# Grouped-query decode attention with a bilinear feed-forward block: query weights loaded as one chunk, output weights in two loads, gate, up and down weights in fewer pieces

## The chip, the cores and the metric

The kernel runs on one core of a Trainium2 chip. The metric is the device time of one execution in microseconds (us), the median of several runs. All data are 32-bit floats.

## What is computed

One token is decoded. The cut reference, with B = Sq = 1, D = 512, 32 query heads in 8 groups, head size 128, Sk = 65536 cached positions and F = 1792:

```python
q = (layernorm(x) @ wq)                  # 512 x 4096
p = softmax(q . k_cache * 128 ** -0.5)   # 4 query heads share one of 8 K/V heads
h = x + (p . v_cache) @ wo               # 4096 x 512
n = layernorm(h)
y = h + ((n @ w_gate) * (n @ w_up)) @ w_down
```

K and V have 268 MB each; wq and wo 8.4 MB each, gate and up together 7.3 MB, w_down 3.7 MB. Every byte is used once.

## The kernel before, in words

**Chunks.** K and V are read in 64 chunks of 128 partitions x 16384 values (8192 KB, one row of 64 KB per partition). Each of the 8 heads has four K chunks and then four V chunks. Even chunks go to the buffer `kv[0]`, odd ones to `kv[1]`. SP issues every load; before a chunk it waits for the semaphore `free`, which DVE raises when PE has finished with that buffer.

**One chunk on PE.** `windows` (L359) multiplies 32 windows of 512 columns, each with its own 32 columns of the stationary tile `st`, into four row blocks of one bank of `ps`. Each window is two matmul records in the trace, so a chunk is 64 records. A window's operand in `st` is zero but for the columns wanted, so one chunk loop serves K, V, gate and up, and w_down. PE runs one loop over a pair of chunks (`pe_pair`, `pe_chunks`, `pe_second`, `pe_rest`); two registers, head `hr` and pair `ur`, choose the branch.

**A head.** At its start (L391 to L400) PE multiplies the normalized x with the head's 1024 KB of wq (8 records), DVE copies the row `qrow`, PE turns it into columns, and DVE spreads them over `qx` and `st` (L224 to L234). The softmax runs between the K and the V chunks. At the end (`pe_sum`) PE divides out the sum, multiplies with the head's wo, and DVE adds to `acc`. The wq of the next head and the wo of this one come in one load of 2048 KB (L148), issued when DVE has raised `wf`.

**The end.** The last V chunk comes in four pieces (L158). Then SP loads gate and up into `kv[0]` in four pieces with gaps (L162, L164): 3584 of every 4096 columns are filled. It loads w_down into `kv[1]` in pieces of 6, 3, 1, 1, 1, 1 and 1 chunks of 512 columns (L167 to L172). PE and DVE do the layer norm (`pe_norm`, L295 to L315), the 32 windows of gate and up, then `pe_glu`: a matmul for the variance, four transposes of the result, and a matmul into `attn` whose result nobody reads (L430). DVE forms the products (L323 to L336). The first 9 chunks of w_down go through 12 windows, the last 5 through `final` (L370), and `add` (L479) adds `res`, which holds the window sum times the inverse deviation plus `acc` (L340). DVE copies the sum to `y` (L492) and SP stores it.

**Order.** Each engine's order is written out by hand; queues are served in order. A piece has its own semaphore; where before and after differ in the number of pieces, GpSimd raises the unused ones in advance (L133).

```python
take(pe_e, qt)
windows(0, 0, 16, s_k0)
windows(0, 16, 24, s_k16)
windows(0, 24, 28, s_k24)
windows(0, 28, 32, s_k28).then_inc(kd, 1)
```

Of the kernel before, what the change touches and what calls it, by code (L numbers as in the profile page):

```python
# [5 lines left out]
ALU = mybir.AluOpType  # L6
AX = mybir.AxisListType

P = 128
# [33 lines left out]
def body(nc, xr, kvd, wq0, wqo, wo7, gu, wd, out):  # L43
# [11 lines left out]
    sel_h, sel_q, sel_1 = (tile(n, P, w) for n, w in (("sel_h", REP), ("sel_q", 4), ("sel_1", 1)))  # L55
# [21 lines left out]
    gu_sb, uf, y = tile("gu_sb", P, 512), tile("uf", P, 2, 2, 4, 2), tile("y", P, 256)  # L77
# [18 lines left out]
    s_k0, s_k16, s_k24, s_k28 = (sem(f"s_k{i}") for i in (0, 16, 24, 28))  # L96
    s_v0, s_v8, s_v16, s_v24, s_v28 = (sem(f"s_v{i}") for i in (0, 8, 16, 24, 28))
    s_wq, s_w = sem("s_wq"), sem("s_w")
    s_wd = [sem(f"s_wd{i}") for i in range(NC - SIDE)]
    s_xr = sem("s_xr")  # L100
    late, s_act, s_pool, s_y, s_a, s_out = (sem(n) for n in ("late", "s_act", "s_pool", "s_y", "s_a", "s_out"))
    gu_t = kv[0].rearrange("p (k x) -> p k x", k=KT)[:, :, 0:2 * F]
# [18 lines left out]
    sp.dma_start(wq_sb, wq0).then_inc(s_wq, 16)  # L121
# [11 lines left out]
    for p, w, n in ((s_k16, 16, 0), (s_k24, 16, 0), (s_k28, 16, 0), (s_v8, 17, 0),  # L133
                    (s_v16, 16, -1), (s_v24, 16, -1), (s_v28, 16, -1)):
        pool_e.sem_inc(p, w * (end // 2 + n))
    for t in (o_pad, f_pad, sel_pad, acc, y):
        c_pads = pool.tick(pool_e.memset(t, 0.0))
    pool_e.wait_ge(s_act, 1).then_inc(s_pool, 1)
    pool_e.br("fin")

    even(0)
    odd(1)
    for g in range(2, 6):
        take(sp, free)
        (odd if g % 2 else even)(g)
    with nc.Fori(0, LAST, engines=SP_ONLY) as h:
        take(sp, wf)
        sp.dma_start(wqo_sb, wqo[h]).then_inc(s_w, 16)  # L148
        with nc.Fori(0, 2 * NT, 2, engines=SP_ONLY) as c:
            for i, put in enumerate((even, odd)):  # L150
                take(sp, free)
                put(c + (h * (2 * NT) + 6 + i))
    take(sp, wf)
    sp.dma_start(wo_sb, wo7).then_inc(s_w, 16)
    take(sp, free)
    even(end - 2)
    take(sp, free)
    for lo, hi, p in ((0, 16, s_v0), (16, 24, s_v16), (24, 28, s_v24), (28, 32, s_v28)):  # L158
        cs = slice(lo * 512, hi * 512)
        sp.dma_start(kv[1][:, cs], kvd[end - 1][:, cs]).then_inc(p, 16)  # L160
    take(sp, free)
    for lo, hi, p in ((0, 2, s_k0), (2, 3, s_k16)):  # L162
        sp.dma_start(gu_t[:, lo:hi], gu[:, lo:hi]).then_inc(p, 16)
    for cs, p in ((slice(0, 2048), s_k24), (slice(2048, 2 * F), s_k28)):  # L164
        sp.dma_start(gu_t[:, 3, cs], gu[:, 3, cs]).then_inc(p, 16)
    take(sp, free)
    sp.dma_start(  # L167
        wd_t[:, 0:8 * D].rearrange("p (r x) -> p r x", r=2)[:, :, 0:3 * D],
        wd[:, 0:6 * D].rearrange("p (r x) -> p r x", r=2)).then_inc(s_v0, 16)
# [39 lines left out]
    dve_e.tensor_copy(xn, ps[0][:, 0:KT]).then_inc(tok, 3)  # L209
# [3 lines left out]
    with nc.Fori(0, HKV, engines=DVE_ACT):  # L213
# [9 lines left out]
        take(dve_e, pd)  # L223
        dve_e.tensor_copy(qrow, ptp[0][0:1, :]).then_inc(tok, 1)  # L224
        take(dve_e, pd)
        dve_e.sem_inc(wf, 1)
        q4 = sm[0][:, 0:REP]
# [58 lines left out]
        for half, p in ((0, tok), (1, s_a)):  # L286
            cs = slice(half * 256, half * 256 + 256)
            dve_e.scalar_tensor_tensor(  # L288
                out=acc[:, cs], in0=attn[:, cs], scalar=1.0, in1=acc[:, cs], op0=ALU.mult, op1=ALU.add,
                accum_out=rsum[:, half:half + 1]).then_inc(p, 1)  # L290
# [4 lines left out]
    dve_e.memset(st[:, :, 0:2], 0.0).then_inc(own, 1)  # L295
# [7 lines left out]
    def centred(o, a):  # L303
# [3 lines left out]
    hj = st.rearrange("p (j k t) c -> p t k j c", j=4, k=KT)  # L307
    centred(hj[:, 0, :, :, 0], acol.unsqueeze(2).to_broadcast([P, KT, 4]))
    centred(hj[:, 1, :, 0:3, 1], acol.unsqueeze(2).to_broadcast([P, KT, 3])).then_inc(qt, 1)
# [5 lines left out]
        out=ln_s3, in0=ln_s3, scalar1=KT * EPS, scalar2=None, op0=ALU.add).then_inc(tl, 1)  # L315
    take(dve_e, kd)
    for half in range(2):
        cs = slice(half * 256, half * 256 + 256)
        dve_e.tensor_copy(gu_sb[:, cs], ps[0][:, cs]).then_inc(tl, 1)
    sj = st.rearrange("p (j r) c -> p r j c", j=4)[:, :, :, 0]  # L320
    gux = [t.rearrange("p (a b j x) -> p a b j x", a=2, b=2, j=4)[:, 0, :, :, 0:2] for t in ptp]
    take(dve_e, pd, 2)
    mine(dve_e.tensor_copy(uf[:, 0], gux[0]))  # L323
    dve_e.tensor_tensor(
        out=sj[:, 0:2, :], in0=gux[0][:, :, :, 0], in1=uf[:, 0, :, :, 1], op=ALU.mult).then_inc(qt, 1)
    dve_e.reciprocal(ln_r3, sm[0][:, 0:1])
    take(dve_e, pd)
    mine(dve_e.tensor_copy(uf[:, 1], gux[1]))
    dve_e.tensor_tensor(
        out=sj[:, 2, :], in0=gux[1][:, 0, :, 0], in1=uf[:, 1, 0, :, 1], op=ALU.mult)  # L330
    for o, g, u in ((f_pad[:, 0:1, 0], gux[0][:, 0, 3:4, 0], uf[:, 0, 1, 3:4, 0]),
                    (f_pad[:, 1:4, 0], gux[1][:, 1, 0:3, 0], uf[:, 1, 1, 0:3, 1]),
                    (f_pad[:, 4:5, 0], gux[1][:, 0, 3:4, 0], uf[:, 1, 1, 3:4, 0])):
        i = dve_e.scalar_tensor_tensor(
            out=o, in0=g, scalar=ln_r3[:, 0:1], in1=u, op0=ALU.mult, op1=ALU.mult)
    i.then_inc(s_v8, 1)  # L336
    take(dve_e, kd)
    for half in range(2):
        cs = slice(half * 256, half * 256 + 256)
        dve_e.scalar_tensor_tensor(  # L340
            out=res[:, cs], in0=ps[1][:, cs], scalar=ln_r3[:, 0:1], in1=acc[:, cs],
            op0=ALU.mult, op1=ALU.add).then_inc(tl, 1)
# [39 lines left out]

    hr, ur = (pe_e.alloc_register(n) for n in ("h", "u"))
# [5 lines left out]
    pe_e.br("pe_head")  # L389
    block("pe_head")  # L390
    pe_e.wait_ge(tok, 3)  # L391
    for k in range(KT):
        i = mm(ptp[0][0:1, :], xn[:, k:k + 1], wq_sb[:, k, :], start=(k == 0), stop=(k == KT - 1))  # L393
    i.then_inc(pd, 1)
    pe_e.wait_ge(tok, 4)
    for r in range(REP):
        i = pe_e.transpose(sm[0][:, r:r + 1], qrow[0:1, r * P:(r + 1) * P], ident[0:1, 0:1])  # L397
        if r == 1:
            i.then_inc(tok, -4)
    i.then_inc(pd, 1)  # L400
# [45 lines left out]
    windows(1, 16, 24, s_v16)  # L446
    windows(1, 24, 28, s_v24)
# [94 lines left out]
```

## Time and profile before

| what | value |
|---|---|
| median of 3 runs | 1308.67 us (1308.66 to 1308.84) |
| profiled execution, first to last instruction (span) | 1307.4 us |
| median less span | 1.27 us |
| PE busy | 686.2 us (52%) |
| DVE busy | 111.6 us (9%) |
| ACT busy | 54.9 us (4%) |
| bytes moved by DMA | 564.72 MB, 432 GB/s over the span |

The profile gives no time of its own for the profiled execution but the span, so what lies around the span is taken as the difference to the median. A row of the timeline has start, duration, engine, line, operation, the tile written and those read, the number of merged instructions, and in brackets the idle time before it with what ended it. PE is the matmul side of TensorE, PEld its weight loads. PEclk is the granted clock: 1.00 is 2.4 GHz, 0.50 is 1.2 GHz.

### The profile page before, as it was taken

The numbers are of one execution on the slowest core, as the hardware profiler recorded it, in microseconds if no ns is written. First come the engines' busy times: TensorE is split into PE (matmuls) and PEld (weight loads), VectorE is DVE, ScalarE is ACT, GpSimd is POOL, SyncE is SP. The second block draws the span as 40 slices with busy tenths as digits, with TensorE's granted clock in tenths as the row PEclk, the third lists the DMA queues.
The fourth block names the chain that finished last, engine by engine and source line by source line (L and its number), as shares of the span: only waits on it lengthen the run. The fifth ranks groups of instructions, "written<-read, shape, count | busy, mean of one in ns | idle before, by whom it ended". The sixth has DMA issues, their size and how long they took to land. (4 is left out here: it accounts for less than half of the span.)

```text
span 1307.4 us, 10833 instructions
## 1 busy us (share of the span) xinstructions
PE 686.2 (52%) x4610; PEld 191.5 (15%) x4610; DVE 111.6 (9%) x286; ACT 54.9 (4%) x106; POOL 2.7 (0%) x12
## 2 busy tenths in 40 slices
PE   4456364453654545553554636535566445545557
PEld 1011111110111111111110211101111111111112
DVE  1000010100101001000010101001010010100101
ACT  0000000000000000000000000000000000000000
POOL 0000000000000000000000000000000000000000
PEclk8676796776976768767787767868677677877679
DMA  9999999999999999999999999999999999999999
GB/s 417 421 445 429 437 447 419 449 417 449 417 449 417 449 417 449 421 445 427 439 439 427 449 417 449 417 449 417 449 417 449 417 434 440 441 437 429 447 408 382
DMA packets 12850, 564.72 MB, mean 432 GB/s; under 512 B 1409, under 2 KB 1457, under 8 KB 2610
## 3 DMA queue, kind: packets, MB, share of 16 engines
q1 hardware_dynamic: 12848, 564.71, 99.8%
q10 hardware_dynamic: 2, 0.00, 0.0%
HBM read 564.66 MB, written 0.05 MB: 432 GB/s over the span
## 5 line engine op out<-in xcount | busy, mean ns | idle before, releaser
L364 PE MATMUL ps<-kv,st 128*32 128x512 f32 x4184 | 591.0, 728 | 534.6 <-DMA kv<-in_kv 520.1
L364 PEld LDWEIGHTS ps<-kv,st 128*32 128x32 f32 x4184 | 146.7, 131 | 962.3 <-DMA kv<-in_kv 568.1
L242 DVE TENSOR_REDUCE mx<-sc 128x1 f32<-128x512 f32 x32 | 21.9, 686 | 535.9 <-DVEq L107 535.9
L414 PE MATMUL ptp<-ident,ex 128*128 128x128 f32 x128 | 27.3, 372 | 19.8 <-ACT ex L220 19.5
L216 ACT COPY sc<-ps 128x512 f32<-128x512 f32 x32 | 18.8, 586 | 444.6 <-ACTq L107 444.5
L274 DVE TENSOR_TENSOR orow<-ps,orow 128x512 f32<-128x512 f32 x16 | 11.1, 691 | 298.3 <-DVEq L107 298.3
L220 ACT ACTIVATE ex<-sc,nbias 128x512 f32<-128x512 f32 x32 | 22.8, 714 | 304.4 <-ACTq L107 304.4
L393 PE MATMUL ptp<-wqo_sb,xn 128*1 128x512 f32 x64 | 30.4, 620 | 6.4 <-DVE acc L288 5.0
L216 ACT ACT_TABLE_LOAD x8 | 10.3, 1283 | 441.5 <-ACTq L107 441.5
L261 DVE COPY st<-ptp 128x512 f32<-128x512 f32 x32 | 22.1, 692 | 44.5 <-DVEq L107 44.5
L414 PEld LDWEIGHTS ptp<-ident,ex 128*128 128x128 f32 x128 | 20.2, 188 | 22.9 <-ACT ex L220 22.8
L407 PE MATMUL sm<-ident,m 128*1 128x128 f32 x16 | 4.5, 283 | 27.2 <-DVE m L244 17.6
L277 DVE TENSOR_TENSOR orow<-ps,orow 128x256 f32<-128x256 f32 x16 | 6.0, 419 | 129.3 <-DVEq L107 129.3
L272 DVE COPY orow<-ps 128x512 f32<-128x512 f32 x8 | 5.5, 692 | 102.0 <-DVEq L107 102.0
L461 PE MATMUL attn<-wqo_sb,o_pad 128*32 128x512 f32 x64 | 8.5, 605 | 5.9 <-DVE o_pad L284 5.9
L409 PE MATMUL sm<-ones,mexp 1*128 1x1 f32 x32 | 6.9, 281 | 6.7 <-DVE mexp L251 6.7
L393 PEld LDWEIGHTS ptp<-wqo_sb,xn 128*1 128x1 f32 x64 | 4.9, 85 | 30.9 <-issue 18.1
L224 DVE COPY qrow<-ptp 1x512 f32<-1x512 f32 x8 | 5.4, 679 | 29.7 <-DVEq L107 29.7
L457 PE MATMUL ptp<-ident,orow 128*128 128x128 f32 x32 | 6.1, 300 | 3.0 <-DVE orow L277 3.0
L407 PEld LDWEIGHTS sm<-ident,m 128*1 128x1 f32 x16 | 1.3, 79 | 41.8 <-DVE m L244 24.9
L288 DVE SCALAR_TENSOR_TENSOR acc<-attn,acc 128x256 f32<-128x256 f32 x16 | 6.2, 421 | 10.8 <-DVEq L107 10.8
L397 PE MATMUL sm<-ident,qrow 1*128 1x1 f32 x32 | 3.2, 201 | 7.1 <-DVE qrow L224 7.1
(84 smaller groups left out, 78.4 us busy)
## 6 DMA issues: line engine op xcount, KB each, us to landing
wqo_sb<-in_wqo SPq DMA_DIRECT2D x7, 2048.0 KB, 32.9
kv<-in_kv SPq DMA_DIRECT2D x1, 4096.0 KB, 22.2
kv<-in_gu SPq DMA_DIRECT2D x1, 3584.0 KB, 17.6
kv<-in_kv SPq DMA_DIRECT2D x1, 2048.0 KB, 26.7
kv<-in_kv SPq DMA_DIRECT2D x2, 1024.0 KB, 29.7
kv<-in_gu SPq DMA_DIRECT2D x1, 1792.0 KB, 21.4
kv<-in_wd SPq DMA_DIRECT2D x1, 1536.0 KB, 19.0
kv<-in_wd SPq DMA_DIRECT2D x5, 256.0 KB, 20.5
```

The lines of the kernel that those rows point to most:

```text
L216: act_e.copy(sc[s], ps[s % 2]).then_inc(ad, 1)
L220: act_e.activation(ex[s - n], sc[s], AF.Exp, bias=nbias[:, 0:1], scale=SCALE, accum_out=sums[:, s:s + 1]).then_inc(atok[s - n], 1)
L242: dve_e.tensor_reduce(out=mx[:, s:s + 1], in_=sc[s], axis=AX.X, op=ALU.max).then_inc(own, 1)
L261: dve_e.tensor_copy(st[:, :, 0:16].rearrange("p g (b h) -> p b g h", h=REP), ptp[n % 2].rearrange("p (b g h) -> p b g h", b=4, h=REP)).the ...
L274: mine(dve_e.tensor_tensor(out=orow, in0=ps[n % 2], in1=orow, op=ALU.add))
L288: dve_e.scalar_tensor_tensor(out=acc[:, cs], in0=attn[:, cs], scalar=1.0, in1=acc[:, cs], op0=ALU.mult, op1=ALU.add, accum_out=rsum[:, hal ...
L364: i = mm(ps[buf][32 * j:32 * j + 32, :], st[:, 8 * j + r, :], kv[buf][:, w * 512:(w + 1) * 512], start=(r == 0), stop=(r in (2, 3, 7)), sk ...
L393: i = mm(ptp[0][0:1, :], xn[:, k:k + 1], wq_sb[:, k, :], start=(k == 0), stop=(k == KT - 1))
L409: mm(sm[0][:, 0:1], mexp.rearrange("p g h -> p (g h)"), ones[0:1, 0:1], start=True, stop=True).then_inc(pd, 1)
L414: i = pe_e.transpose(ptp[half][:, b * P:(b + 1) * P], ex[half][:, b * P:(b + 1) * P], ident)
L457: i = pe_e.transpose(ptp[1][:, b * P:(b + 1) * P], orow[:, b * P:(b + 1) * P], ident)
L461: i = mm(attn[32 * r:32 * r + 32, :], o_pad[:, r, :], wo_sb[:, r, :], start=True, stop=True)
```

## The change

- **Query weights.** All of wq is one chunk of 8192 KB, the first load into `kv[1]`. It goes through the chunk loop once ahead of the heads: `st` gets the normalized x (`diagonal(0)`), the eight rows of queries come out of one bank, and a new PE block `pe_pick` turns and gathers them with `sel_8` into `q_all`. The heads lose their q matmuls, the row copy and the transposes. The second K chunk is issued only when wq has left `kv[1]` (an added wait on `free`).
- **Output weights.** wo comes in two loads of 4096 KB, heads 0 to 3 at the start and 4 to 7 when DVE has raised `wf` four times. GpSimd waits for each and raises `tw` by four. PE picks one of four quarter tiles by the register `wr`.
- **Gate and up** are packed without gaps, at windows 4 to 31 of `kv[0]`, in two pieces of 20 and 8 windows. `pe_pick` replaces the transposes of `pe_glu`; the unread matmul L430 is gone. The variance matmul moves ahead of the gate and up windows, and two matmuls there put `acc` into `pva`.
- **w_down** comes in pieces of 8, 3, 2 and 1 chunks; 11 chunks go through the windows, 3 through `final`. `res` is now a plain copy, because the inverse deviation is multiplied into the products.
- **Last V chunk** in two pieces instead of four.

```diff
-SIDE = 9
+SIDE = 11
-    sp.dma_start(wq_sb, wq0).then_inc(s_wq, 16)
+    sp.dma_start(kv[1], wq).then_inc(s_v0, 16)
...
     even(0)
+    take(sp, free)
     odd(1)
-    for g in range(2, 6):
-        take(sp, free)
-        (odd if g % 2 else even)(g)
-    with nc.Fori(0, LAST, engines=SP_ONLY) as h:
-        take(sp, wf)
-        sp.dma_start(wqo_sb, wqo[h]).then_inc(s_w, 16)
-        with nc.Fori(0, 2 * NT, 2, engines=SP_ONLY) as c:
+    for half, pairs in ((0, end // 4), (1, end // 4 - 2)):
+        if half:
+            take(sp, wf, HKV // 2)
+        sp.dma_start(wo_sb, wo[half]).then_inc(s_wo, 16)
+        with nc.Fori(0, 2 * pairs, 2, engines=SP_ONLY) as c:
             for i, put in enumerate((even, odd)):
                 take(sp, free)
-                put(c + (h * (2 * NT) + 6 + i))
+                put(c + (2 + half * (end // 2) + i))
...
+    pieces((0, 16, 32), 0, kv[1], kvd[end - 1], (s_v0, s_v16))
+    pieces((0, 20, 28), 4, kv[0], gu, (s_k0, s_k24))
+    pieces((0, 8, SIDE), 0, wd_t, wd, (s_v0, s_v8))
+    for lo, hi, p in ((SIDE, NC - 1, s_wd[0]), (NC - 1, NC, s_wd[1])):
+        sp.dma_start(wd_t[:, (lo + 1) * D:(hi + 1) * D], wd[:, lo * D:hi * D]).then_inc(p, 16)
...
+    dve_e.tensor_copy(diagonal(0), spread(ps[0][:, 0:KT], 8)).then_inc(qt, 1)
+    take(dve_e, kd, 2)
+    dve_e.sem_inc(free, 1)
+    columns(ps[1])
+    mine(dve_e.tensor_copy(q_all, picked.rearrange("p b c -> p c b")))
...
     take(pe_e, qt)
-    windows(0, 0, 16, s_k0)
-    windows(0, 16, 24, s_k16)
-    windows(0, 24, 28, s_k24)
-    windows(0, 28, 32, s_k28).then_inc(kd, 1)
-    pe_e.br_eq(hr, HKV, on_true="pe_glu", on_false="pe_second")
+    windows(0, 0, 24, s_k0)
+    windows(0, 24, 32, s_k24).then_inc(kd, 1)
+    pe_e.br_eq(hr, HKV, on_true="pe_pick", on_false="pe_second")
```

How the instructions move is shown at three places. First SP's loads from the start into the steady loop (`in_` is the DRAM tensor, the size is partitions x values). Before:

```order
L121 DMA wqo_sb<-in_wq 128x2048
L116 DMA kv<-in_kv 128x16384
L119 DMA kv<-in_kv 128x16384
L116 DMA kv<-in_kv 128x16384
L119 DMA kv<-in_kv 128x16384
L116 DMA kv<-in_kv 128x16384
L119 DMA kv<-in_kv 128x16384
L146 UNCONDITIONAL_BRANCH
L148 ISA
L148 DMA wqo_sb<-in_wqo 128x4096
```

Changed:

```order
L118 DMA kv<-in_wq 128x16384
L113 DMA kv<-in_kv 128x16384
L116 DMA kv<-in_kv 128x16384
L147 DMA wo_sb<-in_wo 128x8192
L148 UNCONDITIONAL_BRANCH
L113 ISA
L113 DMA kv<-in_kv 128x16384
```

The load of wq is eight times as long and shares its buffer with the second K chunk; the load per head is gone, and a load of 4096 KB stands once ahead of each half of the chunks. Second, SP's last loads. Before:

```order
L160 DMA kv<-in_kv 128x8192
L160 DMA kv<-in_kv 128x4096
L160 DMA kv<-in_kv 128x2048 x2
L163 DMA kv<-in_gu 128x2x3584
L163 DMA kv<-in_gu 128x3584
L165 DMA kv<-in_gu 128x2048
L165 DMA kv<-in_gu 128x1536
L167 DMA kv<-in_wd 128x2x1536
L170 DMA kv<-in_wd 128x1536
L172 DMA kv<-in_wd 128x512 x5
```

Changed:

```order
L158 DMA kv<-in_kv 128x8192 x2
L158 DMA kv<-in_gu 128x10240
L158 DMA kv<-in_gu 128x4096
L158 DMA kv<-in_wd 128x4096
L158 DMA kv<-in_wd 128x1536
L165 DMA kv<-in_wd 128x1024
L165 DMA kv<-in_wd 128x512
```

Fifteen loads became eight. Third, PE behind the last windows of w_down, up to the end (`pva` holds the result, `f_pad` the products). Before:

```order
L374 MATMUL pva<-kv,f_pad 32x256 [waits s_wd0]
L374 MATMUL pva<-kv,f_pad 32x256
L374 MATMUL pva<-kv,f_pad 32x256 [waits s_wd1]
L374 MATMUL pva<-kv,f_pad 32x256
L481 MATMUL pva<-res,sel_pad 32x256 [waits tl]
L374 MATMUL pva<-kv,f_pad 32x256 [waits s_wd2]
L374 MATMUL pva<-kv,f_pad 32x256
L481 MATMUL pva<-res,sel_pad 32x256 [waits tl]
L374 MATMUL pva<-kv,f_pad 32x256 [waits s_wd3]
L374 MATMUL pva<-kv,f_pad 32x256
L488 UNCONDITIONAL_BRANCH
L374 MATMUL pva<-kv,f_pad 32x256 [waits s_wd4]
```

Changed:

```order
L372 MATMUL pva<-kv,f_pad 32x256 [waits s_wd0]
L372 MATMUL pva<-kv,f_pad 32x256 x3
L377 MATMUL pva<-res,sel_pad 32x256 [waits tl] x2
L486 UNCONDITIONAL_BRANCH
L372 MATMUL pva<-kv,f_pad 32x256 [waits s_wd1]
L372 MATMUL pva<-kv,f_pad 32x256
```

The two additions of `res` now stand directly ahead of the last chunk's matmuls, where three chunks' matmuls, two of them with waits, used to stand behind the first addition.

## Rows read from the trace of the kernel before

**Rows 1.** the page: its DMA line by slices, and the packets of the whole span.
```profile
DMA  9999999999999999999999999999999999999999
...
DMA packets 12850, 564.72 MB, mean 432 GB/s; under 512 B 1409, under 2 KB 1457, under 8 KB 2610
```
**Rows 2.** windows, middle of the span; at the end PEclk, DMA share, GB/s.
```profile
600.00:1100.00 500.00, 257.92 (x1755) 72.47 (x1755) 39.91 (x95) 21.52 (x43) 0.00 (x0) 0.75 1.01 435
```
**Rows 3.** timeline, PE, chunks 0, 1, 5 and 6: start, us, what, idle before.
```profile
24.92 9.39 PE L364 MATMUL ps<-kv,st 128*32 128x512 f32 x64 [9.20 <-DMA kv<-in_kv]
...
44.26 9.96 PE L364 MATMUL ps<-kv,st 128*32 128x512 f32 x64 [9.95 <-DMA kv<-in_kv]
...
121.65 8.81 PE L364 MATMUL ps<-kv,st 128*32 128x512 f32 x64 [9.40 <-DMA kv<-in_kv]
...
145.87 8.65 PE L364 MATMUL ps<-kv,st 128*32 128x512 f32 x64 [11.12 <-DMA kv<-in_kv]
```
**Rows 4.** DMA issues: how many, KB each (left out: 8192), median us to landing.
```profile
wqo_sb<-in_wqo SPq DMA_DIRECT2D x7, 2048.0 KB, 32.9
...
kv<-in_kv SPq DMA_DIRECT2D x63, 29.3
...
kv<-in_wd SPq DMA_DIRECT2D x5, 256.0 KB, 20.5
```
**Rows 5.** the chain that ended last: start, us, what.
```profile
1280.60 18.98 DMA kv<-in_wd
...
1305.37 0.42 DVE y L492
```
**Rows 6.** timeline, PE and its weight loads, last value chunk to the end.
```profile
1271.46 8.77 PE L364 MATMUL ps<-kv,st 128*32 128x512 f32 x64 [2.10 <-PEq L107]
...
1278.86 0.13 PEld L364 LDWEIGHTS ps<-kv,st 128*32 128x32 f32 x4 [0.39 <-DMA kv<-in_kv]
...
1287.36 3.64 PE L364 MATMUL ps<-kv,st 128*32 128x512 f32 x32 [2.26 <-DMA kv<-in_gu]
...
1291.59 1.92 PE L364 MATMUL ps<-kv,st 128*32 128x512 f32 x16 [0.59 <-DMA kv<-in_gu]
...
1294.04 1.06 PE L364 MATMUL ps<-kv,st 128*32 128x512 f32 x8 [0.52 <-DMA kv<-in_gu]
...
1295.94 1.06 PE L364 MATMUL ps<-kv,st 128*32 128x512 f32 x8 [0.84 <-DMA kv<-in_gu]
...
1299.62 2.88 PE L364 MATMUL ps<-kv,st 128*32 128x512 f32 x24 [0.30 <-DMA kv<-in_wd]
...
1301.44 0.16 PEld L364 LDWEIGHTS ps<-kv,st 128*32 128x32 f32 x8 [0.80 <-DMA kv<-in_wd]
...
1302.32 1.08 PE L374 MATMUL pva<-kv,f_pad 128*32 128x256 f32 x8
...
1304.64 0.20 PEld L374 LDWEIGHTS pva<-kv,f_pad 128*32 128x32 f32 x4 [0.23 <-DMA kv<-in_wd]
```
**Rows 7.** page, part 5: the heads' q matmuls: busy, mean ns | idle before.
```profile
L393 PE MATMUL ptp<-wqo_sb,xn 128*1 128x512 f32 x64 | 30.4, 620 | 6.4 <-DVE acc L288 5.0
```
**Rows 8.** timeline, DVE, the normalization, gate/up and the residual.
```profile
1286.74 0.15 DVE L314 TENSOR_SCALAR ln_s<-ln_s 128x1 f32<-128x1 f32 x1
...
1297.21 0.76 DVE L319 COPY gu_sb<-ps 128x256 f32<-128x256 f32 x2 [10.31 <-DVEq L107]
...
1298.60 0.17 DVE L324 TENSOR_TENSOR st<-ptp,uf 128x8 f32<-128x8 f32 x1
...
1302.71 0.88 DVE L340 SCALAR_TENSOR_TENSOR res<-ps,ln_r,acc 128x256 f32<-128x256 f32 x2 [3.07 <-DVEq L107]
```
**Rows 9.** windows around the last value chunk and the gate/up stage.
```profile
1272.40:1275.80 3.40, 3.40 (x24) 1.15 (x20) 0.00 (x0) 0.00 (x0) 0.00 (x0) 0.54 0.94 400
...
1287.30:1297.00 9.70, 7.69 (x65) 1.73 (x65) 0.00 (x0) 0.00 (x0) 0.00 (x0) 1.00 1.00 425
1297.00:1299.50 2.50, 1.95 (x9) 0.90 (x8) 1.69 (x10) 0.00 (x0) 0.00 (x0) 1.00 1.01 423
```

More of the change, by code (lines that the diff above doesn't have):

```diff
@@ L40, in tick, with body @@
         return self.n
-def body(nc, xr, kvd, wq0, wqo, wo7, gu, wd, out):
+def body(nc, xr, wq, kvd, wo, gu, wd, out):
     pe_e, dve_e, act_e, pool_e, sp = nc.tensor, nc.vector, nc.scalar, nc.gpsimd, nc.sync
@@ L208, in body, with diagonal, spread, columns @@
     take(dve_e, pd)
-    dve_e.tensor_copy(xn, ps[0][:, 0:KT]).then_inc(tok, 3)
+    def diagonal(lo):
+        return bass.AP(tensor=st.tensor, offset=33 * lo, ap=[list(st.ap[0]), [256, KT], [33, 8 - lo]])
+    def spread(a, n):
+        return a.unsqueeze(2).to_broadcast([P, KT, n])
+    def columns(src):
+        for half in range(2):
+            cs = slice(half * 256, half * 256 + 256)
+            dve_e.tensor_copy(gu_sb[:, cs], src[:, cs]).then_inc(tl, 1)
+        take(dve_e, pd)
+    picked = ptp[0][:, 0:32].rearrange("p (b c) -> p b c", b=4)
+    dve_e.tensor_copy(diagonal(0), spread(ps[0][:, 0:KT], 8)).then_inc(qt, 1)
[3 more added lines that the diff above has]
+    mine(dve_e.tensor_copy(q_all, picked.rearrange("p b c -> p c b")))
     o_blocks = bass.AP(tensor=ptp[1].tensor, offset=0, ap=[list(ptp[1].ap[0]), [1, REP], [132, 4], [32, 4]])
     qd = qx.rearrange("p (j x) -> p j x", j=4)
-    with nc.Fori(0, HKV, engines=DVE_ACT):
+    with nc.Fori(0, HKV, engines=DVE_ACT) as head:
         for s in range(NT):
@@ L222, in body @@
                     accum_out=sums[:, s:s + 1]).then_inc(atok[s - n], 1)
[L223 to L227, printed above, removed]
+        q4 = q_all[:, head, :]
         dve_e.tensor_copy(
@@ L285, in body @@
         take(dve_e, pd)
-        for half, p in ((0, tok), (1, s_a)):
+        dve_e.sem_inc(wf, 1)
+        for half in range(2):
             cs = slice(half * 256, half * 256 + 256)
@@ L318, in body @@
         cs = slice(half * 256, half * 256 + 256)
[L319 to L342, printed above, removed]
+        dve_e.tensor_copy(res[:, cs], ps[1][:, cs]).then_inc(tl, 1)
     dve.n += 1
@@ L388, in body @@
     pe_e.reg_mov(hr, 0)
-    pe_e.br("pe_head")
-    block("pe_head")
[L391 to L400, printed above, removed]
+    pe_e.reg_mov(wr, 0)
+    pe_e.reg_mov(ur, 2 * NT)
+    pe_e.br("pe_second")
+    block("pe_pick")
+    for b in range(4):
+        if b % 2 == 0:
+            pe_e.wait_ge(tl, 1 + b // 2)
+        i = mm(ptp[0][:, 8 * b:8 * b + 8], gu_sb[:, b * P:(b + 1) * P], sel_8, start=True, stop=True)
+        if b == 2:
+            i.then_inc(tl, -2)
+    i.then_inc(pd, 1)
+    pe_e.br_lt(hr, HKV, on_true="pe_head", on_false="pe_second")
+    block("pe_head")
     pe_e.reg_mov(ur, 0)
@@ L474, in body @@
     mm(sm[1][:, 0:2], neg_mean, rsum, start=True, stop=True).then_inc(pd, 1)
+    for g in range(2):
+        add(g, acc, True)
+    pe_e.wait_ge(tok, 1)
+    mm(sm[0][:, 0:1], mean_m, ln_s3, start=True, stop=True).then_inc(pd, 1)
     pe_e.br_eq(hr, HKV, on_true="pe_chunks", on_false="pe_other")
```

181 lines of the change are left out of this document (87 added, 94 removed).

## The prediction

> **What bounds the kernel now.** I read the page first. The DMA engines are at nine tenths or more in every slice, and 564.72 MB moved in 12850 packets [rows 1]. The windows confirm it: from 600 to 1100 us the DMA share is 1.01 at 435 GB/s [rows 2]. Next comes PE at the landings. Chunks 0 and 1 start on PE 19.34 us apart (24.92, 44.26), each behind an idle time of over 9 us that ended with the chunk's DMA [rows 3]. So a chunk of 8192 KB passes in 19.34 us, 2.42 us per 1024 KB, and PE needs only 8.65 to 9.96 us for it. A chunk lands 29.3 us after its issue [rows 4]. Less the 19.34 us of its own transfer, about 10 us of other loads are still ahead of it when it is queued. PE, DVE and ACT work in the shadow of the loads. The time is the bytes at that pace, a start and a tail. The change moves the same bytes, so only three things can move the time: the pace of small loads, a hole in the queue, and the work after the last landing.
>
> The tail is in the chain that ended last: the loads of w_down from 1280.60, then PE, then DVE's copy to `y` at 1305.37 [rows 5]. The last load's weights start on PE at 1304.64 [rows 6]. I call that landing E; the copy starts at E + 0.73. I count back from E below.
>
> **The loads.** Before there are 87 loads: 1 of wq, 63 whole chunks, 4 pieces of the last, 7 of wqo, 1 of wo, 4 of gate and up, 7 of w_down. After there are 74: 1 + 63 + 2, 2 of wo, 2 and 4. What a load costs beyond its bytes shows at the end, where each landing has a PE row: 1287.36, 1291.59, 1294.04, 1295.94, 1299.62, 1301.44, and the last at 1304.64 [rows 6]. Between the first and the last, 10 loads with 1792 + 1024 + 768 + 1536 + 768 + 5 x 256 = 7168 KB took 17.28 us. At the chunks' pace that is 16.92 us, so a load costs 0.036 us more. One wqo load between two chunks agrees: 121.65 to 145.87 is 24.22 us [rows 3], against 24.18 for 10240 KB. Thirteen loads fewer save 13 x 0.036 = **0.5 us**. Bounds from single loads there: the one of 1792 KB cost nothing, the third one of gate and up 0.09 us. That gives a saving from 0 to 1.2 us. I take the mean, since the loads removed are of all these kinds.
>
> The Trainium skill's page "DMA: Bandwidth & Descriptors" (Anatomy of one DMA) gives each DMA a fixed cost of about 2.0 us beside its bytes. By that, 13 loads fewer would save 26 us. Here the trace disagrees: five loads of 256 KB [rows 4] landed in 1304.64 - 1301.44 = 3.20 us, 0.64 us each.
>
> **The start.** The 1024 KB of wq and chunk 0 had landed by 24.92; at 2.42 us per 1024 KB the loads began at about 3.2. After, wq lands at 22.5. PE takes up to 9.96 us for a chunk [rows 3], so SP issues the second K chunk at about 33. Chunk 0 holds the DMA engines until 41.9. So the added wait on `free` has 9 us of cover and costs nothing. Behind it on SP are the first load of wo and the chunk after; neither is late, as they are queued before the second K chunk has landed. The wait on `wf` in the middle stands behind chunk 33 on SP. When it begins, chunk 32 is in flight with about 10 us to go and chunk 33 is whole. The head's last steps, which it waits for, lie within the 6.66 us counted below from the last V matmul to `ln_s`. Nothing there either. GpSimd waits for wo and has nothing else to do until the end.
>
> **The heads.** They lose the q matmuls (64 records, 30.4 us of busy time in all [rows 7], 3.8 us a head), the row copy and the transposes. All of it lies inside waits of over 9 us for the next chunk: worth nothing. An earlier `free` only queues a load earlier behind one that is running.
>
> **The last stages, counted from E.** With 2.42 us per 1024 KB and 0.036 us per load, the changed loads land at E - 0.64 (12 and 13 of the 14 chunks of w_down), E - 1.89 (9 to 11), E - 3.74 (the first eight), E - 8.61 and E - 13.48 (gate and up), and the last V chunk at E - 25.60.
>
> - *Last V chunk.* Before, the last of four pieces landed at 1278.86, four windows were left, and the matmuls ended at 1271.46 + 8.77 = 1280.23, E - 24.41 [rows 6]. After, 16 windows (32 records) follow the last landing: 3.64 us by the row with 32 records, so E - 21.96, later by 2.45.
> - *Norm.* `ln_s` was ready at 1286.89 [rows 8], 6.66 us after the last V matmul. After that is E - 15.30, and the variance matmul now ahead of gate and up adds about 0.5. PE is ready at E - 14.8, 1.3 us before the first piece lands. No cost.
> - *Gate and up.* 16 records more cost 3.64 - 1.92 us, or 0.1075 each [rows 6]. The first piece has 48 records, 5.16 us, to E - 8.32, behind the second landing. Then 16 records, 1.92 us, to E - 6.40; DVE starts 0.21 later, as it did at 1297.21 [rows 8]. Before, 1.56 us passed from there to the product at 1298.77. After, `pe_pick` needs the second copy too (0.38 more), and a second product comes ahead of the signal (0.17): 2.11 us, E - 4.08. The first eight chunks of w_down land at E - 3.74. Hidden, with only **0.34 us** to spare.
> - *Down.* The 24 window records run as before, 2.88 us [rows 6], to E - 0.86. DVE starts 0.21 later and copies two halves in 0.76, to E + 0.1; before, `res` was ready at 1303.59, E - 1.05 [rows 8]. PE works off the two-chunk load's 8 records from E - 0.64 to about E + 0.2 (0.1 us apart, from 8 in 1.08 us [rows 6]), then four for `res`, to E + 0.6, then the last four and the 0.73 us up to the copy: E + 1.3. Before it was E + 0.73. So the tail grows by **0.6 us**. Bounds: 0, if the two additions cost no more than they did when they stood among the last loads, and 1.1, if none of these records overlap (16 x 0.1 more behind `res`, less the 0.5 counted).
>
> **Sum.** 1307.4 - 0.5 + 0.6 = 1307.5 us of span. The median of the runs stands 1.27 us above the span, so I forecast **1308.8 us**: no change. The bounds of the two terms give 1307.5 to 1309.8. A measurement of this kernel can tell a difference of some 0.2%, 2.6 us, from none.
>
> **Rivals.**
>
> 1. *Half clock under gate and up (slower).* The place is the 64 records of that stage. Nothing else there has slack: 0.34 us. PE had just been idle for 2.10 us when it took up the last V chunk [rows 6], and the granted clock was then 0.54, the 1.2 GHz level, from 1272.4 to 1275.8 [rows 9]. Behind 2.26 us of idle ahead of gate and up it stayed at 1.00 [rows 6, 9]. So it can go either way. After the change, thin work stretches from E - 21.96 to E - 13.48, 8.5 us where it was 7.1, and the unread matmul L430 behind the stage is gone. The Trainium skill's page "TensorE: Matmul & The Clock Gate" (Part 1) calls the throttled state the default which only activity releases; it leans to this rival. Price: 64 records from an idle engine took 8.65 to 9.96 us [rows 3], against 7.08 above. Less the slack that is 1.2 to 2.5 us: 1310.0 to 1311.3, say **1310.6**. It passes 0.2% when the 24 records of w_down are slow too (24 x 0.1075 = 2.6 us more: 1313.2).
> 2. *Each load costs more than its mean (faster).* With 0.09 us each and a tail that does not grow: 1308.67 - 1.2, **1307.5**. For it: the saving is certain in sign. Against it: the 1792 KB load cost nothing.
> 3. *The queue runs dry.* If PE or SP were later than the covers above (9 us at the start, 10 us and a chunk at `wf`), each us beyond is a us lost: 1312 and more. The rows give no reason.
> 4. *The fixed cost of a DMA is on the path after all.* At 0.2 us for each of 13 loads, the least that would show, 1306.1 or less. The 0.64 us per 256 KB speak against it. The Trainium skill's page on DMA, named above, leads to this rival.
>
> **How the numbers follow.** Forecast 0.57; rival 1 0.22, of which 0.06 beyond 0.2%; rival 2 0.14; rival 3 0.04; rival 4 0.03. Faster by over 0.2%: rival 4, 0.03. Slower: 0.06 + 0.04 = 0.10. The rest, 0.87, is within. The range is 1307.5 to 1310.9: it holds the forecast with its bounds, rival 2, and most of rival 1, and leaves out about 0.15.
>
> **What would show it.** The DMA share stays at 1.0 to the last landing, and chunks land 19.3 us apart from the second on. The last landing comes about 0.5 us earlier in the span than 1304.64. The gate and up matmuls take some 7.1 us at a granted clock of 1.00, and the first windows of w_down wait for their load, not for DVE. The copy to `y` starts 1.3 us behind the last landing. I am wrong if a chunk waits for its issue, if PE shows half clock behind the last V chunk, or if the last landing moves by over 1.2 us.

## The result, and the profile after

The changed kernel takes **1313.73 us** (median of 5 runs, 1312.95 to 1315.58) against 1308.74 us for the kernel before: a ratio of 1.0038, 95% interval 1.0026 to 1.0051. It is 5.0 us slower, forecast was no change, and the time lies above the range. The profiled execution took 1313.87 us with a span of 1312.2.

The page, its DMA line, packets and queues:

```profile
DMA  9999999999999999999999999999999999999997
...
DMA packets 10723, 564.73 MB, mean 430 GB/s; under 512 B 1201, under 2 KB 1249, under 8 KB 1634
...
q1 hardware_dynamic: 10720, 564.71, 99.4%
q8 instruction: 1, 0.02, 0.0%
```

The DMA engines are as busy as before [rows 1], but the last slice has fallen to 7, and there is a queue that the kernel before does not have: q8, one packet of instructions.

The chain that ended last (start, us, what):

```profile
1305.04 2.95 PE ps L361 x22
1307.99 0.91 PE pva L372 x7
...
1310.15 0.42 DVE y L490
```

Before, a load of w_down stood in it [rows 5]. Now there is no load at all: PE runs behind the data. The timeline of PE shows from where on (start, us, what, idle before):

```profile
23.82 8.95 PE L361 MATMUL ps<-kv,st 128*32 128x512 f32 x64 [15.15 <-DMA kv<-in_wq]
...
43.13 9.53 PE L361 MATMUL ps<-kv,st 128*32 128x512 f32 x64 [8.54 <-DMA kv<-in_kv]
...
1279.80 5.58 PE L361 MATMUL ps<-kv,st 128*32 128x512 f32 x32 [5.21 <-DMA kv<-in_kv]
...
1288.10 1.06 PE L451 MATMUL attn<-wo_sb,o_pad 128*32 128x512 f32 x8 [1.29 <-DVE o_pad L291]
...
1292.64 0.59 PE L475 MATMUL sm<-ln_s,mean_m 128*128 128x1 f32 x2 [0.56 <-DVE ln_s L320]
1293.15 9.16 PE L361 MATMUL ps<-kv,st 128*32 128x512 f32 x64
1302.98 1.06 PE L393 MATMUL ptp<-sel,gu_sb 128*128 128x8 f32 x8 [0.67 <-DVE gu_sb L212]
1305.04 3.04 PE L361 MATMUL ps<-kv,st 128*32 128x512 f32 x24 [1.00 <-PEq L104]
```

The loads are late from the first on: wq at 23.82 and chunk 0 at 43.13, forecast 22.5 and 41.9. The last V piece lands 1.3 us later than forecast, and its 32 records take 5.58 us, not 3.64. Gate and up wait for no load; their 64 records take 9.16 us, not 7.08. The first 24 of w_down wait for DVE, not for their load. The windows give the granted clock under the V piece, the norm, and the two halves of gate and up (ahead of DMA share and GB/s):

```profile
1279.80:1285.40 5.60, 5.60 (x33) 1.32 (x33) 0.00 (x0) 0.00 (x0) 0.00 (x0) 0.65 0.86 373
1285.40:1293.10 7.70, 4.66 (x26) 2.27 (x26) 3.50 (x16) 0.00 (x0) 0.00 (x0) 0.84 0.99 427
1293.15:1297.40 4.25, 4.25 (x21) 0.97 (x24) 0.17 (x1) 0.00 (x0) 0.00 (x0) 0.50 1.01 432
1297.40:1302.30 4.90, 4.90 (x48) 1.19 (x40) 0.00 (x0) 0.00 (x0) 0.00 (x0) 1.00 0.99 418
```

0.50 is the 1.2 GHz level; before, this stage stood at 1.00 [rows 9].

The packet records of the trace show why the loads are late. In the middle of the wq load, at 14.7 us, 16384 bytes of instructions pass through one DMA engine in 0.92 us, and the data packet behind them takes 2.93 us where those on the other engines take 2.42. From then on that engine is behind. Each load leaves sixteen landing marks in the trace, one of each engine: fifteen of the last load's stand at 1303.95 to 1304.28, one at 1305.27. PE waits for all sixteen (the last V piece: fifteen marks by 1278.79, the last at 1279.76, PE starts at 1279.80), so every later landing has this engine's 1.0 us in it.

### The profile page after: what moved, and what is told of

Same layout as the page of the kernel before. It is cut to its first block, busy times and chain, and to the rows that moved or that the text cites. A ratio compares the mean times of both kernels' runs of the same rounds, so it can differ in the third digit from the quotient of the medians.

```text
span 1312.2 us, 10763 instructions
## 1 busy us (share of the span) xinstructions
PE 677.6 (52%) x4584; PEld 189.5 (14%) x4584; DVE 107.3 (8%) x277; ACT 54.9 (4%) x106; POOL 3.5 (0%) x13
## 5 line engine op out<-in xcount | busy, mean ns | idle before, releaser
L361 PE MATMUL ps<-kv,st 128*32 128x512 f32 x4248 | 612.3, 741 | 556.3 <-DMA kv<-in_kv 538.1
L451 PE MATMUL attn<-wo_sb,o_pad 128*32 128x512 f32 x64 | 10.1, 707 | 9.1 <-DVE o_pad L291 9.1
L407 PEld LDWEIGHTS sm<-ones,mexp 1*128 1x128 f32 x32 | 5.7, 221 | 9.4 <-DVE mexp L258 8.5
L231 ACT ACTIVATION_READ_ACCUMULATOR ex<-sc,nbias 128x1 f32 x32 | 6.0, 186 | 0.0
L241 DVE COPY st<-qx 128x1024 f32<-128x1024 f32 x8 | 5.5, 694 | 1.2
```

The source lines that it names most:

```text
L231: act_e.activation(ex[s - n], sc[s], AF.Exp, bias=nbias[:, 0:1], scale=SCALE, accum_out=sums[:, s:s + 1]).then_inc(atok[s - n], 1)
L407: mm(sm[0][:, 0:1], mexp.rearrange("p g h -> p (g h)"), ones[0:1, 0:1], start=True, stop=True).then_inc(pd, 1)
L451: i = mm(attn[32 * r:32 * r + 32, :], o_pad[:, r, :], wo_sb[:, n, r, :], start=True, stop=True)
```

## The experiments

Three suspects: records left behind late pieces (A: the last V chunk; C: gate and up), the half clock (D), and late loads (B, later F and G: the instruction fetch). Medians are of 5 to 11 runs; the kernel before had 1308.75 to 1308.92 beside them. "Record" is one matmul record of PE. Each kernel has the trace of one execution; where its time lies far from the median, it is given.

### The pieces put back in the changed kernel

```diff
...
-    pieces((0, 16, 32), 0, kv[1], kvd[end - 1], (s_v0, s_v16))
+    pieces((0, 16, 24, 28, 32), 0, kv[1], kvd[end - 1], (s_v0, s_v16, s_v24, s_v28))
...
```

> The changed kernel with the last V chunk in four pieces (16, 8, 4 and 4 windows) as before; gate and up stay in two. Theory A (matmuls left behind the last V landing set the end): 8 records follow the last landing instead of 32, so the V matmuls end about 4 us earlier than the 1285.4 of the changed kernel's trace, the gate/up stage starts when its first piece lands (near 1292) instead of 1293.15, and the time falls by 1.1 to 3 us, to 1310.7 to 1312.6. Theory B (the loads themselves end later and nothing else matters): no change, 1313.5 to 1314. Theory C (only the large first piece of gate/up matters): no change either.

**1313.91 us**, ratio 1.0041 (1.0027 to 1.0055): nothing gained. In the traced execution, the fastest of the five (1311.75 us), the V records end at 1280.7, 4.7 us earlier, but gate and up wait for their first piece until 1291.79, and their 64 records take 8.72 us.

```diff
...
-    pieces((0, 20, 28), 4, kv[0], gu, (s_k0, s_k24))
+    pieces((0, 12, 20, 24, 28), 4, kv[0], gu, (s_k0, s_k16, s_k24, s_k28))
...
```

> The changed kernel with gate and up in four pieces (12, 8, 4 and 4 windows of 512 columns, that is up to window 16, 24, 28 and 32); the last V chunk stays in two. Theory A: PE reaches gate/up only at 1293.15, when the first 20 windows have landed anyway, so nothing changes: within 0.5 us of 1313.7. Theory C (the large first piece holds PE up): the time falls by 2 us or more. Theory B: no change.

**1312.36 us**, 1.0026 (1.0015 to 1.0036): 1.4 us less by the medians, within the spread of the runs (1310.88 to 1314.09). Gate and up still start at 1292.40, behind the V piece and the norm.

> Both cuts: the last V chunk and gate/up in four pieces each. Theory A: PE follows the landings through the whole end; the first windows of w_down wait for their load again, and the copy to y starts about 1.3 us behind the last landing, so 1309.0 to 1310.3. Theory B: 1313.5 or more. If only one of the two cuts mattered, this equals the better of the two single runs.

Both edits together: **1312.97 us**, 1.0030 (1.0017 to 1.0042). Gate and up wait for loads again and run at the full clock, and then the loss moves on to w_down:

```profile
1297.43 1.07 PE L362 MATMUL ps<-kv,st 128*32 128x512 f32 x8 [1.39 <-DMA kv<-in_gu]
...
1302.33 5.33 PE L362 MATMUL ps<-kv,st 128*32 128x512 f32 x24 [2.09 <-DMA kv<-in_wd]
```

24 records take 5.33 us, against 2.88 before [rows 6], and they start 2.7 us later, at a landing. So the clock is left and so are the late loads: 0.9 us of the 2.7 are the late engine's. The first piece of w_down also has 8 chunks instead of 6, which at the chunks' pace is some 1.2 us; no run went back to the old first piece, so its price is not tested.

### Clock

```diff
...
+    for _ in range(6):
+        mm(attn, ones, kv[1][:, 0:512], start=True, stop=True)
...
     windows(1, 16, 32, s_v16).then_inc(kd, 1)
```

> The changed kernel with its pieces as they are, but in the last V chunk PE runs six matmuls (128x512, into a bank that nobody reads then) between the two pieces, so it is not idle for the 5.2 us ahead of the second one. Added work only; no wait is removed. Theory D (the clock: the same pieces would cost little at 2.4 GHz): the 32 records behind the last V landing take 3.6 us instead of 5.6, gate/up takes 7.1 instead of 9.2, and the time falls by 2 to 4 us, to 1309.7 to 1311.7. Theory A without the clock: the pieces cost the same, 1313.5 to 1314, or more if the added matmuls run past the landing.

**1314.40 us**, 1.0042 (1.0029 to 1.0056; runs from 1311.98 to 1317.17), a miss in its aim: the six unread matmuls (last V chunk alone) ran 2.9 us beyond the landing at 1279.81. In the traced execution (1316.84 us) the 32 records then took 3.64 us, but gate and up took 9.41:

```profile
1282.72 3.64 PE L361 MATMUL ps<-kv,st 128*32 128x512 f32 x32
...
1294.91 9.41 PE L361 MATMUL ps<-kv,st 128*32 128x512 f32 x64
```

So filling the idle time ahead of the V records does not keep the clock up under gate and up, which stand behind the norm.

```diff
...
     add(g, acc, True)
+    for _ in range(2):
+        mm(attn, mean_m, wo_sb[:, 0, 0, :], start=True, stop=True)
```

> The changed kernel with the last V chunk and gate and up in four pieces each (as e3_v4_gu4), and four unread matmuls: two in the norm behind its additions, two behind gate and up ahead of w_down. Theory D (what is left of the loss is the half clock under the 24 records of w_down): these take 2.9 us instead of 5.3, and the time falls from 1313.0 to 1310.4 us. Against it (the clock falls all the same, or the landings alone set the end): 1312.5 to 1313 us.

**1311.27 us**, 1.0019 (1.0010 to 1.0028): 1.7 us less than e3_v4_gu4, of 2.6 expected. In the traced execution (1312.71 us) the 24 records took 2.78 us.

> The kernel before without its unread matmul at L430, which stands between gate and up and w_down; nothing else is changed. Theory D: the 24 records of w_down run at the half clock, 5.3 us instead of 2.9, 1310.4 to 1311.3 us. If the clock does not hang on this matmul: 1308.8 us, no change.

```diff
-    mm(attn, mean_m, wo_sb[:, 0, :], start=True, stop=True)
```

**1308.87 us**, 1.0000 (0.9991 to 1.0009). Theory D fell here in this form: without L430 the 24 records still took 2.88 us.

### One part of the change in the kernel before

```diff
...
-    for lo, hi, p in ((0, 16, s_v0), (16, 24, s_v16), (24, 28, s_v24), (28, 32, s_v28)):
+    for lo, hi, p in ((0, 16, s_v0), (16, 32, s_v16)):
```

> The kernel before with only the last V chunk in two pieces of 16 instead of four (16, 8, 4, 4). Theory A (the 32 records behind the last landing set the end): the V matmuls end at 1282.2 to 1284.3 and gate and up start 2 to 4 us later, but their last pieces land at 1294.0 and 1295.9 and half of the delay is caught up at the full clock: 1308.8 to 1309.8 us. If the clock falls under gate and up as well: 1310.5 to 1311.5.

**1308.90 us**, 1.0006 (0.9997 to 1.0015), but of two kinds: six runs at 1308.58 to 1308.90 and five at 1310.80 to 1311.54. The profile is one of the latter: its 32 records took 6.32 us, gate and up 8.71. So the two-piece V load costs nothing in some runs and some 2 us in others. In the traced one of the others the clock was down; that it stayed up in the fast six is likely, but no trace shows one of them.

```diff
...
-    for lo, hi, p in ((0, 2, s_k0), (2, 3, s_k16)):
+    for lo, hi, p in ((0, 3, s_k0), (3, 4, s_k24)):
```

(the two loads of the last quarter go, too)

> The kernel before with only gate and up in two pieces (three quarters, one quarter) instead of four. Theory C (a first piece that lands late leaves 64 records behind it): gate and up start at 1291.4 and end at 1298.5 at the full clock or 1300.7 at the half clock, 1.5 to 3.7 us later than before, w_down's first 24 records 0.5 to 3 us later; 1309.3 to 1311.7 us. If it is hidden: 1308.8.

**1311.65 us**, 1.0022 (1.0013 to 1.0031), no run below 1311.22. This is the largest loss that one part of the change makes alone: 2.8 us.

> The kernel before with the last V chunk in two pieces and gate and up in two, as in the changed kernel; everything else of before is kept (no instruction fetch, w_down in its seven loads). Theories A and C (what is left behind the landings makes the loss): the V matmuls end 2.5 to 4 us later, gate and up 1 to 3 us later, w_down's first load at 1299.6 no longer sets its start, and the time is 1309.8 to 1311.5 us. If the pieces cost nothing by themselves: 1308.8 us.

Both: **1311.48 us**, 1.0016 (1.0007 to 1.0025). The two prices don't add: in both runs gate and up start at their landing (1291.40 here, 1291.77 in b2_gu2), and a later V end only shortens the idle time ahead of it (4.23 us, 6.80 in b2_gu2).

> b2_gu2 with six unread matmuls in the norm, where PE has 6.8 us of idle time ahead of gate and up; they read what lies in the on-chip memory and load nothing. Theory D (the idle time lets the clock fall, and the half clock makes most of the price of the two-piece gate and up): the 64 records run at the full clock in 7.1 us from 1291.7, w_down's first 24 records start 2.1 to 2.7 us earlier than in b2_gu2, 1309.8 to 1310.2 us. Theory C alone (the late first piece is the price, whatever the clock): 1311.4 to 1311.7, as b2_gu2.

```diff
...
+    block("pe_warm")
+    mm(attn, mean_m, wo_sb[:, 0, :], start=True, stop=True)
+    pe_e.reg_add(ur, ur, 1)
+    pe_e.br_lt(ur, 6, on_true="pe_warm", on_false="pe_ready")
...
```

**1309.98 us**, 1.0010 (1.0001 to 1.0019); two of the 11 runs still took 1311.7 to 1311.8. Only the idle time was filled. The timeline of PE in b2_gu2, gate and up and the first records of w_down:

```profile
1291.77 9.73 PE L362 MATMUL ps<-kv,st 128*32 128x512 f32 x64 [6.80 <-DMA kv<-in_gu]
...
1303.75 2.78 PE L362 MATMUL ps<-kv,st 128*32 128x512 f32 x24
```

and in b7_gu2_warm, with the unread records ahead:

```profile
1284.96 5.40 PE L476 MATMUL attn<-wqo_sb,mean_m 128*128 128x512 f32 x12
1291.92 7.07 PE L362 MATMUL ps<-kv,st 128*32 128x512 f32 x64 [1.56 <-DMA kv<-in_gu]
...
1301.24 2.78 PE L362 MATMUL ps<-kv,st 128*32 128x512 f32 x24
```

The same start and the same records, 9.73 against 7.07 us. The windows say that this is the clock; b2_gu2, idle time and the records behind it:

```profile
1284.90:1291.70 6.80, 0.07 (x1) 0.00 (x0) 1.21 (x7) 0.00 (x0) 0.00 (x0) 0.65 0.99 426
1291.80:1297.00 5.20, 5.20 (x28) 1.26 (x32) 0.00 (x0) 0.00 (x0) 0.00 (x0) 0.50 0.98 416
```

and b7_gu2_warm:

```profile
1284.90:1291.70 6.80, 5.46 (x15) 2.23 (x13) 1.21 (x7) 0.00 (x0) 0.00 (x0) 1.00 0.98 420
1291.90:1299.00 7.10, 7.08 (x65) 2.06 (x65) 0.00 (x0) 0.00 (x0) 0.00 (x0) 1.00 0.98 415
```

Of the 2.8 us, 1311.65 - 1309.98 = 1.7 are the clock (D); the 1.1 left at the full clock go to the records behind a later piece (C). The two traced executions lie further apart than the medians (1312.65 and 1310.18 us).

### The instruction fetch

> The changed kernel with the windows of the wq chunk written out straight behind pe_main, so that PE's program does not jump far ahead at its start. Theory F (an instruction fetch that the jump causes goes through one DMA engine in the middle of the wq load, and that engine stays late by about 1.3 us to the end): the packet on the instruction queue is gone from that place, the last data lands about 1.2 us earlier, 1312.4 us. Theory B (the landings are later for another reason, such as fewer and larger loads): the packet moves or goes, the landings stay, 1313.7 us. The tail behind the landings is unchanged, so either way it stays over 1311 us and the granted clock in the tail is half for most of gate and up.

```diff
-    pe_e.reg_mov(ur, 2 * NT)
-    pe_e.br("pe_second")
+    pe_e.reg_mov(ur, 0)
+    take(pe_e, qt)
...
+    windows(1, 16, 32, s_v16).then_inc(kd, 1)
+    pe_e.br("pe_pick")
```

**1312.58 us**, 1.0033 (1.0021 to 1.0045). The packet moved to 41.2 us; the late engine's last mark still stands at 1305.14, the next at 1304.30. Theory F, that the jump makes the fetch, fell. The time came out near the one of theory F (1312.4 us) by chance, as the late engine stayed: in the traced execution, the fastest (1311.45 us), gate and up took 7.27 us, at the full clock.

> The changed kernel with PE's blocks written in another order (pe_second and pe_rest straight behind pe_main, then pe_pick, pe_head, pe_pair, pe_soft, pe_chunks); the same instructions run in the same order but for one more branch behind every K chunk. Theory F: without a far jump at the start there is no instruction fetch at 15 us, all DMA engines end within 0.5 us of each other at 1304.2, and the landings are 1.1 us earlier; the time falls from 1313.7 to 1312.5 us. If the fetch only moves, as in e5_inline, the late engine stays and the time is as there, 1312.6 us, or that of the changed kernel.

**1312.16 us**, 1.0027 (1.0017 to 1.0038). The same: packet at 41.5 us, one engine at 1305.88, the next at 1304.66. Here the V records ran at the full clock (3.64 us), gate and up did not (8.77).

> The kernel before with 50 matmuls that are never executed between pe_main and pe_head, so that PE's first jump passes over them as the changed kernel's first jump passes over some 50 matmuls; nothing that runs is changed. Theory F (a far jump of PE makes an instruction fetch on one DMA engine, and every landing waits for that engine from then on): a 16 KB packet on the instruction queue in the first 20 us, one DMA engine that ends about 1 us behind the others, the last landing at about 1305.6 us, 1309.8 us. Against it: no packet, or a packet that is made up for by the end, 1308.8 us.

**1308.87 us**, 1.0001 (0.9992 to 1.0010), inconclusive: no branch reaches those matmuls, so they were dropped from the program that ran. It is one more measurement of the kernel before.

> The kernel before with 12 more matmuls at the end of PE's program, behind a branch that is never taken; all that runs is unchanged but for that one branch at the start. Theory G (PE's program is now longer than what is there at the start, so that a part of it is fetched in the run, through one DMA engine, and every landing waits for that engine to the end): a 16 KB packet on the instruction queue before 60 us, one DMA engine about 1 us behind the others at the end, the last landing at about 1305.5 us, the time 1309.7 us. Against it (the length does nothing): no packet, 1308.8 us.

```diff
-    pe_e.br("pe_head")
+    pe_e.br_eq(hr, 99, on_true="pe_dead", on_false="pe_head")
```

(and the 12 matmuls of pe_dead behind pe_down)

**1309.92 us**, 1.0009 (1.0000 to 1.0018): 1.1 us slower, though all that runs is unchanged but for one branch. The page has `q8 instruction: 2`; the first packet passed at 34.1 us (the second at 1306.1, behind the data), and one engine's last mark stands at 1305.67, the next at 1304.62. PE's weight loads in the timeline show the landings:

```profile
1288.39 0.16 PEld L364 LDWEIGHTS ps<-kv,st 128*32 128x32 f32 x8 [2.60 <-DMA kv<-in_gu]
...
1305.71 0.17 PEld L374 LDWEIGHTS pva<-kv,f_pad 128*32 128x32 f32 x4 [0.26 <-DMA kv<-in_wd]
```

1.03 and 1.07 us later than 1287.36 and 1304.64 [rows 6]. Theory G holds: the length of PE's program makes the fetch, and the fetch costs 1.1 us.

> The changed kernel with one block of wo matmuls instead of four, so that PE's program is 12 matmuls shorter; the same number of instructions runs, but every head multiplies by the first head's quarter of the loaded wo (that part of the computation is changed). Theory G: no packet on the instruction queue, all DMA engines end within 0.5 us of each other near 1304.2 us, and the tail, which hangs on PE, starts 1 us earlier: 1312.3 to 1312.7 us, against 1313.7. Against it: the packet stays or the time does.

```diff
-    pe_e.br_lt(wr, 2, on_true="pe_low", on_false="pe_high")
...
+    for r in range(REP):
+        i = mm(attn[32 * r:32 * r + 32, :], o_pad[:, r, :], wo_sb[:, 0, r, :],
+               start=True, stop=True)
...
```

**1310.20 us**, 1.0013 (1.0004 to 1.0022). The packet of 16384 bytes is gone (64 bytes at the very start are all the instructions in its records), and the last mark stands at 1304.43. The load of wq lands 22.0 us behind its issue, 23.0 in the changed kernel, and PE takes up wq at 22.77 and chunk 0 at 42.06, not at 23.82 and 43.13:

```profile
q14 instruction: 1, 0.00, 0.0%
...
kv<-in_wq SPq DMA_DIRECT2D x1, 22.0
```

The gain is 3.5 us, not the 1.0 to 1.4 expected. Two rows of the profile say where more came from:

```profile
1287.59 1.06 PE L446 MATMUL attn<-wo_sb,o_pad 128*32 128x512 f32 x8 [0.83 <-DVE o_pad L291]
...
1292.41 7.07 PE L361 MATMUL ps<-kv,st 128*32 128x512 f32 x64
```

PE's idle time ahead of the wo records is 0.83 us instead of 1.29: two branches fewer. And gate and up ran at the full clock, though the V records ahead of the norm had taken 6.34 us at 0.57 of it. The runs reach from 1309.30 to 1312.57, so the clock probably does not come out the same in each; what decides it there is open.

### Together

> e6_keep with the windows of the wq chunk written out as in e5_inline. If the pieces, the clock and the instruction fetch together make the loss: 1308.7 to 1309.4 us, no slower than the kernel before. If theory F is wrong, as e6_keep.

**1310.42 us**, 1.0013 (1.0004 to 1.0022). The packet stayed (39.0 us), so it shows the clock and the pieces alone. It differs from e6_keep by the written-out windows only; the 0.9 us between them is less than the spread of either.

> The blocks of e8_order, the pieces of e3_v4_gu4, and one unread matmul instead of e6_keep's two at each of the two places. If the fetch is gone and the granted clock stays full under gate and up and w_down: gate and up wait for their landings, w_down ends 1 us earlier than in e7_all, 1308.6 to 1309.6 us. If one unread matmul is not enough for the clock: 1310.5 to 1313 us.

**1311.43 us**, 1.0019 (1.0010 to 1.0028): one unread matmul at each place was not enough, the 24 records of w_down took 4.31 us. The packet stayed here, too (41.2 us).

> e6_keep (last V chunk and gate and up in four pieces each, two unread matmuls in the norm and two ahead of w_down) with one block of wo matmuls as in e10_short (the same part of the computation is changed). If the pieces, the clock and the instruction fetch make the whole loss but for the longer path through pe_pick: last landing at 1304.3, 1309.0 to 1309.8 us. If there is more: 1310.4 us, as e7_all, or above.

**1309.47 us**, 1.0006 (0.9997 to 1.0015). Pieces, clock and fetch put right leave 0.6 us or nothing. Part of it may be the cure: in the traced execution (1310.29 us) w_down's first piece landed at 1300.54, but the unread matmuls held its records back.

```profile
1298.46 3.60 PE L401 MATMUL attn<-wo_sb,mean_m 128*128 128x512 f32 x4
1301.98 2.78 PE L362 MATMUL ps<-kv,st 128*32 128x512 f32 x24
```

No version beat the kernel before.

## Why the prediction was wrong

Two steps failed. The forecast priced the records behind the last V landing and those of gate and up at the full clock, 3.64 and 7.08 us; they took 5.58 and 9.16, partly at the half clock. And it let only three things move the time; the length of PE's program was a fourth, and its fetch made every landing 1.0 us later.

- **The loads, -0.5 us: right in sign.** Without the late engine the changed kernel's last mark stands at 1304.28, and in e10_short at 1304.43, against 1304.60 before: 0.2 to 0.3 us earlier. The size is not sure: e8_order has the same loads and stands at 1304.66. The step that failed is "only three things can move the time". A fourth did: the program grew (four blocks of wo matmuls), and the fetch took 1.1 us. The 26 us that the prediction sets beside this entered no sum. The Trainium skill's page "DMA: Bandwidth & Descriptors" (Anatomy of one DMA) puts most of its 2.0 us into completion latency, so they do not follow from it.
- **Start wait, heads, `wf`: right.** Chunks 0 and 1 started 19.33 us apart (43.13, 62.46), and from 600 to 1100 us the DMA share was 1.00 at 434 GB/s, against 1.01 at 435 [rows 2].
- **Last V chunk, 3.64 us: failed.** It took 5.58, at 0.65 of the clock behind 5.21 us of idle time. The change itself makes that idle time, as the piece before is half a chunk away. The row of 3.64 [rows 6] stood behind 2.26 us. The traces of the other runs with two V pieces go the same way: 3.64 us behind 1.89, 2.40 and 2.76 us of idle time (b3_v2_gu2, e2_gu4, e8_order), 5.96 to 6.34 behind 4.40 to 4.82 (b1_v2, e5_inline, e10_short).
- **Norm, no cost: failed by little.** From the end of the V records to gate and up passed 7.77 us, 7.2 forecast; 0.46 of it are the two branches that e10_short leaves out. The 1.3 us of slack were eaten by late landing and V records.
- **Gate and up, 7.08 us: the step that decided.** Rival 1 was the right mechanism at the right place, given 0.22, and its price of 1.2 to 2.5 us holds the 1.7 us that b7_gu2_warm measured. The records took 9.16, the first 4.25 us at 0.50 of the clock. I weighed idle times of 2.10 and 2.26 us [rows 6], which went either way, and did not count that the change makes the gaps 5.21 us, or in b2_gu2 6.80. That idle time lowers the clock under gate and up is shown by filling it for b2_gu2 alone. In the changed kernel gate and up stand behind the thin work of the norm, PE busy for 4.66 of 7.70 us; with much the same norm they ran at the full clock in e5_inline and e10_short, and at the half clock in e4_warm, where the gap ahead of the V records was filled. What decides it there stays open. The Trainium skill's page "TensorE: Matmul & The Clock Gate" (Part 1) calls the slow state the default that activity releases; the trace agrees, 0.50 behind 6.80 us of idle time and 1.00 where they were filled.
- **Tail, +0.6 us: not borne out.** It was counted from the last landing, which no longer set the end. From DVE's first copy of gate and up to the copy of `y` passed 1310.15 - 1302.50 = 7.65 us, and in b7_gu2_warm, with the old tail, 1306.73 - 1299.20 = 7.53: next to nothing.
- **Slips that change nothing.** 48 records of gate and up are 3.64 + 16 x 0.1075 = 5.36 us by the prediction's own rows, not 5.16; the total of 7.08 is right. The load that cost 0.09 us more than the pace is the fourth of gate and up (1295.94), not the third, which cost 0.03.

The rows of the tail, in the changed kernel:

```profile
1302.50 0.76 DVE L212 COPY gu_sb<-ps 128x256 f32<-128x256 f32 x2 [8.96 <-DVEq L104]
...
1310.15 0.42 DVE L490 COPY y<-pva 64x256 f32<-64x256 f32 x1 [1.14 <-PE pva L372]
```

and in b7_gu2_warm:

```profile
1299.20 0.76 DVE L317 COPY gu_sb<-ps 128x256 f32<-128x256 f32 x2 [12.30 <-DVEq L107]
...
1306.73 0.42 DVE L497 COPY y<-pva 64x256 f32<-64x256 f32 x1 [1.63 <-PE pva L372]
```

Along PE's path, in the traced execution: 1.26 (landing, 0.97 of it the late engine) + 1.94 (V) + 0.6 (norm) - 1.3 (slack) + 2.08 (gate and up) = 4.6 us. `y` was copied at 1310.15, forecast 1305.44: 4.7. The rivals were priced one by one, each against a slack that another would use up; the sum of them left the range. Of this sum the experiments show the fetch (b6_long), the two-piece gate and up and its clock (b2_gu2, b7_gu2_warm), and all three causes together (e11_short_keep).

## What to carry to other kernels

Cutting this kernel's last loads into fewer pieces saved some hundredths of a us each and took away what kept PE at work between landings: count the idle time that fewer pieces leave ahead of each stage, and price the records behind it at both clocks. Where nothing hides the tail, a few unread matmuls in the gap can pay (1.7 us in b7_gu2_warm), if they end ahead of the landing (in e4_warm they did not). Where the DMA engines set the time, code that is longer by a dozen matmuls is not always free (1.1 us in b6_long): look on the page for an instruction queue that moves 0.02 MB, a packet of 16384 bytes.

## What was not expected of the hardware

- One fetch of 16384 bytes, 0.92 us on one of 16 DMA engines, delayed every landing by 1.0 us to the end of the run: that engine never caught up. The packet stands among the loads of that engine. The Trainium skill's page "Runtime: NRT & Kernel Launch" (Terms) has instruction memory refilled in blocks of 16 KiB; the packet agrees.
- In these runs, whether it comes did not hang on PE's first jump (e5_inline, e8_order) but on the program's length: it came with 12 matmuls added to the kernel before and went with 12 taken from the changed one.
- With two branches fewer ahead of it, PE took up the wo records 0.46 us sooner after DVE's last step (1.29 to 0.83 us of idle time).
- The kernel before stayed within 1308.58 to 1309.64 in all runs, the changed kernel and its variants spread over 1.4 to 5.2 us. Their traced executions have the half clock in different stages; that this makes the spread is likely, but with one trace of each kernel not shown.
